# A fused attention and MLP kernel: setup, PSUM banks, planner's tables and last store changed

## The chip, the core and the metric

The kernel runs on one core of a Trainium2 chip. The metric is the device time of one launch in microseconds (us), the median of several runs; lower is better. Engines: PE (TensorE, matrix products into PSUM), DVE (VectorE), ACT (ScalarE), POOL (GpSimd) and SP, which here issues nearly all DMA transfers and, like every engine, takes its instructions strictly in order.

## The reference

Three blocks follow each other on a batch of 2, 768 positions, 8 heads of 64 (512 columns):

```python
scores = scale * q @ k^T - slope * dist        # keep: first n_global keys, or 0 <= i-j < n_local
a = softmax(where(keep, scores, -1e9)); x = a @ v
xn = (x - mean) / sqrt(var + 1e-6) * g_ln
x = x + relu(xn @ w_ch1) @ w_ch2               # 512 -> 2048 -> 512
h = relu(x^T @ w_tok1) @ w_tok2                # 768 -> 256 -> 768 over positions
u = x + h^T
out = u + relu(u @ w_ch1') @ w_ch2'            # 512 -> 1536 -> 512
```

`n_global` (8 here) and `n_local` (96 here) are inputs, so the kernel reads them at run time.

## The kernel before

The 1536 rows are 12 tiles `T` of 128 rows, six per batch row. `setup_consts` loads the two counts into one partition (`nwords`, one DMA on SP's queue, one on ACT's), spreads them to 128 partitions by a matmul with a row of ones (`nps`) and a copy (`both`), builds distances (`rel`, 512 columns, raised to a huge value where a key lies ahead of the query) and the first tile's masks, and computes a flag that says whether the fast path may run. In the meantime PE runs dummy matmuls (`keep_busy`). All engines then read the flag and branch. A second flag, read after the fast path, says whether a slow general path must run instead; a bounds check goes with each read.

In the fast path nothing is issued in the order of the code. Every operation is entered in a plan with engine, cost, priority, what it reads and writes and which buffers it takes; the planner (`Plan.order`) runs through the plan as a simulation and its order of starts is the order of instructions on each engine. Priorities come from tables of numbers (`SLOT`, `AHEAD`, `HEAD`, `DUE`, `LEAD` and others), and letters in other tables say which engine does a step (`EVX`, `PVE`, `LOA1`, `FE`, ...: A is ACT, V is DVE, G is GpSimd).

`window_tile` enters one tile of attention, four pairs `p` of heads. For a pair PE computes scores (`S`, L451), DVE adds the mask and takes the row's minimum (`low`, L468), ACT the exponential (`ex`, L473), PE turns the probabilities (`T`, L478), ACT or DVE copies them to SBUF (`pt`, L526 or L529), and PE multiplies by V (`PV`, L483), with a column of ones that gives the sum. For T below SPLIT, 6, the products are in fp32; two pairs share a PSUM bank of the pool `t`, and after each second pair DVE adds a small number to the sums, inverts them and scales 128x256 values into `x` (L537 to L539). For T from 6 the probabilities are split in two fp16 parts, and `PT` says pair by pair whether PE turns them (P) or a DMA transpose does (D).

Then a row tile is normalised (`xn`, `xh`), transposed by SP's DMA transpose into `xa` or `xb` (L591), and the MLPs run as three fp16 matmuls per product (L372 to L374). Weights come as raw words: `stg` is loaded (SP), ACT makes `fw` (L755), DVE `wf` (L761), and ACT with DVE or GpSimd the two fp16 parts `wa`/`wb` (L777, L780, L783); some are stored to DRAM (`scr_...`, L736) and reloaded later (L726). A guard checks value ranges; its tiles are cleared by GpSimd (L663).

PSUM has eight banks, two for each of the pools `m`, `s`, `t` and `k`; `BANKS` names the pool for each use. Results of tiles 0 to 9 are stored when they are done, tiles 10 and 11 (`BEHIND`) in a last block behind a prefetch hint for the second branch.

Of the kernel before, what the change touches and what calls it, by code (L numbers as in the profile page):

```python
# [22 lines left out]
P = 128  # L23
# [21 lines left out]
def setup_consts(o, tp):  # L45

    tc, nc, cp = o.tc, o.nc, o.cp
    w = tp.tile([1, 2, 2], I32, name="nwords")
    for i, n in enumerate((o.n_global, o.n_local)):
        (nc.sync, nc.scalar)[i].dma_start(w[:, i, :], n.bitcast(I32).rearrange("(o a) -> o a", o=1))  # L50
# [9 lines left out]
    ones = tp.tile([1, P], F32, name="ones")  # L60
    nc.vector.memset(ones[:], 1.0)
    idle = o.nps.tile([P, 256], F32, name="idle")
    keep_busy(o, idle, BUSY[0])
# [15 lines left out]
    neg = tp.tile([1, 2, 1], F32, name="neg")  # L79
    nc.vector.scalar_tensor_tensor(out=neg[:], in0=w[:, :, 0:1], scalar=0.0, in1=w[:, :, 1:2], op0=ALU.is_lt,  # L80
                                   op1=ALU.add)
    nval = tp.tile([1, 2, 1], F32, name="nval")
# [9 lines left out]
    ng, nl = nval[:, 0, :], nval[:, 1, :]  # L92
# [3 lines left out]
    both = cp.tile([P, 2], F32, name="both")  # L96
    nc.vector.tensor_copy(both[:], ps[:])
    o.ng, o.nl = both[:, 0:1], both[:, 1:2]
# [301 lines left out]
def window_tile(o, plan, prio, T, slot):  # L400
# [33 lines left out]
    if T >= SPLIT:  # L434

        ao = Buf("ao", lambda: o.sm.tile([P, H, 2, D + 1], F32, tag="ao", name="ao", bufs=2))
        sm = Buf("sum", lambda: o.sm.tile([P, H], F32, tag="sum", name="sum", bufs=3))
    mn = Buf("mn", lambda: o.sm.tile([P, H], F32, tag="mn", name="mn", bufs=3))
    x = o.x[T][:].rearrange("p (h d) -> p h d", h=H)
    for p in range(4):  # L440
        k = k0 + p
        if p % 2 == 0:
# [12 lines left out]
            if T < SPLIT:  # L455
                bv = psum_buf(o, "PV", [4, D + 1])
# [23 lines left out]
        def pv(p=p, pt=pt, bv=bv):  # L480
# [50 lines left out]
        if T < SPLIT:  # L531
            op("T", 2 * PVC * n, prio(k + slot["PV"]), pv, r=[(pt, 0), *vkeys], w=[(bv, p % 2)], get=[bv] if p % 2 == 0 else [])
        if T < SPLIT and p % 2 == 1:
            sm = Buf("sum", lambda: o.sm.tile([P, 4], F32, tag="sum", name="sum", bufs=3))

            def scale(p=p, bv=bv, sm=sm):
                nc.vector.tensor_scalar(out=sm.t[:], in0=bv.t[:, :, D], scalar1=1e-9, scalar2=None, op0=ALU.add)  # L537
# [4 lines left out]
            op("V", 0.7, prio(k + slot["inv"]), scale, r=[(bv, 0), (bv, 1)], w=[("x", T, p // 2)], get=[sm])  # L542
# [101 lines left out]
class Guard:  # L644
# [7 lines left out]
    def __init__(self, o, plan):  # L652
# [458 lines left out]
BANKS = {'L1': 'm', 'L2': 'm', 'L2S': 't', 'norm': 'k', 'chain': 'k', 'uT': 't', 'S': 's', 'T': 't', 'PV': 't', 'tok1': 's', 'tok2': 't'}  # L1111
# [5 lines left out]
def store(o, T):  # L1117
    b, t = divmod(T, NT)
    o.nc.sync.dma_start(o.out[b, t * P:(t + 1) * P, :], o.x[T][:])


def rest_pools(o, ctx):
# [15 lines left out]
    o.ps = {p: pool("ps" + p, o.sizes[p], space=PSUM) for p in PSUMS}  # L1138
# [3 lines left out]
def rest(o, ctx, attn, fast):  # L1142
# [136 lines left out]
LEADS, FLEAD = 25.19, 159.37  # L1279
F2LEAD = [-28.4, -27.06]  # L1280
FE, SE = 'VGVVVVGVVGVG', 'GVGGVVVV'
HEAD = 56.45
DUE = [32.72, 16.66, 78.81, 48.03]
EARLY = [42.85, -26.35, 1.23, -4.64]
LEAD = -178.69
EVAC = 20.66
TOK1 = 41.8
TOKW, TOK0 = 247.08, 102.37
# [5 lines left out]
class WindowAttention:  # L1294
# [8 lines left out]
    def ops(self, o, plan, prio):  # L1303
# [23 lines left out]
class GeneralAttention:  # L1327
# [7 lines left out]
    def attend(self, o, ctx):  # L1335
# [16 lines left out]
        for T in range(NTT):  # L1352
# [24 lines left out]
            for h in range(H):  # L1377
# [16 lines left out]
                acc = bank(o, "PV", 512)  # L1394
# [15 lines left out]
def mixer_kernel(ctx, tc, q, k, v, n_global, n_local, g_ln, w1, w2, wt1, wt2, w3, w4, out):  # L1410
# [20 lines left out]
    near = nc.values_load(flag[0:1, 0:1], min_val=0, max_val=1)  # L1431
# [5 lines left out]
    again = nc.values_load(o.again[0:1, 0:1], min_val=0, max_val=1)  # L1437
# [50 lines left out]
```

## Time and profile before

| | us |
|---|---|
| median of 3 runs | 547.12 (547.0 to 549.04) |
| profiled run, whole | 546.87 |
| profiled run, span of its instructions | 545.08 |
| PE busy | 532.0 |
| DVE, ACT, POOL busy | 408.6, 337.1, 163.2 |
| first weight matmul starts | 53.08 |
| last DVE operation starts | 538.77 |

The span runs from the first to the last instruction; 1.8 us lie outside it. Busy matmuls are pipelined, so a matmul's own duration (0.33 us for 384 columns) is longer than the distance to the next one (0.16). A wait is put down to the semaphore that came last.

### The profile page before, as it was taken

How to read it: one execution, taken by the hardware profiler on the slowest of the kernel's cores; microseconds unless marked ns; L12 is line 12 of the kernel's file. 1: busy time of each engine (PE TensorE's matmuls, PEld its weight loads, DVE VectorE, ACT ScalarE, POOL GpSimd, SP SyncE). 2: the span in 40 equal slices, each digit the busy share in tenths (PEclk: the TensorE clock that was granted, in tenths of full speed). 3: DMA queues.
4: the chain of work that ended last, by engine and by line, in shares of the span. 5: the costliest groups of instructions: out<-in, count | busy, mean ns of one | idle time of the engine just before them, and what ended most of it. 6: DMA issues, size and time to landing. Idle time of an engine off the chain costs nothing.

```text
span 545.1 us, 9103 instructions
## 1 busy us (share of the span) xinstructions
PE 532.0 (98%) x3132; PEld 299.7 (55%) x3132; DVE 408.6 (75%) x902; ACT 337.1 (62%) x760; POOL 163.2 (30%) x181
## 2 busy tenths in 40 slices
PE   7989999999999999999999999999999999999995
PEld 5866666666555555555555555455445545555542
DVE  6977998788699632788897898988987786655341
ACT  6988668786976433459948766576685545524210
POOL 2133221223132424253444245324343442220000
PEclk9998999999999999999999999999999999999999
DMA  8898977695998568277319793146745332302012
GB/s 242 267 232 238 294 209 182 202 259 164 208 234 237 207 174 231 97 240 244 97 39 192 186 267 110 40 136 210 268 121 158 92 133 68 113 1 78 2 40 82
DMA packets 99242, 89.81 MB, mean 165 GB/s; under 512 B 58484, under 2 KB 72820, under 8 KB 99188
## 3 DMA queue, kind: packets, MB, share of 16 engines
q1 hardware_dynamic: 99186, 89.15, 57.2%
q8 instruction: 26, 0.43, 0.3%
q14 instruction: 28, 0.23, 0.1%
q10 hardware_dynamic: 2, 0.00, 0.0%
HBM read 61.87 MB, written 17.83 MB: 146 GB/s over the span
## 4 chain that ended last, share of the span: by engine, by line
PE 84%; ACT 6%; DVE 4%; DMA 2%; SPq 1%; issue 1%; POOL 0%; ACTq 0%
PE L L372 11%; PE L L374 11%; PE L L373 11%; PE L2S L372 9%; PE L2S L374 9%; PE L2S L373 9%; PE chain L372 4%; PE chain L374 4%; PE chain L373 4%; PE S L451 3%; DMA stg<-in_moe_w_ch_dram 2%; PE tok L373 2%; PE tok L372 2%; PE tok L374 2%; ACT ex L473 2%; PE T L478 2%
## 5 line engine op out<-in xcount | busy, mean ns | idle before, releaser
L372 PE MATMUL L2S<-wb,h 128*128 128x512 f16 x228 | 86.4, 379 | 0.0
L373 PE MATMUL L2S<-wb,h 128*128 128x512 f16 x228 | 86.4, 379 | 0.0
L374 PE MATMUL L2S<-wb,h 128*128 128x512 f16 x228 | 86.4, 379 | 0.0
L900 DVE SCALAR_TENSOR_TENSOR x<-L2S,x 128x512 f32<-128x512 f32 x57 | 39.2, 688 | 43.0 <-PE L2S L374 42.9
L755 ACT ACTIVATE fw<-stg 128x512 f16<-128x512 bf16 x62 | 47.5, 777 | 20.1 <-DMA stg<-in_moe_w_ch_dram 16.2
L374 PEld LDWEIGHTS <-h 128*128 128x128 f16 x336 | 32.9, 98 | 39.6
L372 PEld LDWEIGHTS <-h 128*128 128x128 f16 x336 | 33.1, 98 | 35.7
L373 PEld LDWEIGHTS <-h 128*128 128x128 f16 x336 | 32.9, 98 | 35.8
L834 POOL TENSOR_TENSOR Q<-wa 128x512 f32<-128x512 f16 x18 | 25.6, 1422 | 74.8 <-DVE sz L834 55.2
L473 ACT ACTIVATE ex<-ex,mn 128x256 f32<-128x256 f32 (+1 forms) x96 | 41.3, 480 | 7.5 <-DVE mn L468 7.4
L761 DVE SCALAR_TENSOR_TENSOR wf<-stg,fw 128x512 uint32<-128x512 uint32 x62 | 45.0, 739 | 0.5 <-ACT fw L755 0.5
L834 POOL TENSOR_TENSOR Q<-Q 128x256 f32<-128x256 f32 x36 | 31.5, 874 | 32.6 <-DVE Q L834 31.2
L372 PE MATMUL L<-wb,h 128*128 128x512 f16 x108 | 40.9, 379 | 0.0
L373 PE MATMUL L<-wb,h 128*128 128x512 f16 x108 | 40.9, 379 | 0.0
L374 PE MATMUL L<-wb,h 128*128 128x512 f16 x108 | 40.9, 379 | 0.0
L372 PEld LDWEIGHTS <-wa 128*128 128x128 f16 x268 | 26.2, 98 | 20.4 <-issue 2.7
L374 PEld LDWEIGHTS <-wa 128*128 128x128 f16 x268 | 26.2, 98 | 17.3
L373 PEld LDWEIGHTS <-wa 128*128 128x128 f16 x268 | 26.2, 98 | 17.3
L364 DVE SCALAR_TENSOR_TENSOR h<-L,h 128x384 f16<-128x384 f32 x40 | 22.1, 553 | 17.4 <-ACT h L358 17.1
L372 PE MATMUL L<-xa,wa 128*128 128x384 f16 x104 | 34.0, 327 | 0.0
L373 PE MATMUL L<-xa,wa 128*128 128x384 f16 x104 | 33.9, 326 | 0.0
L374 PE MATMUL L<-xa,wa 128*128 128x384 f16 x104 | 33.9, 326 | 0.0
(235 smaller groups left out, 1341.2 us busy)
## 6 DMA issues: line engine op xcount, KB each, us to landing
stg<-in_moe_w_ch_dram SPq DMA_DIRECT2D x56, 512.0 KB, 5.5
wa<-scr_1a SPq DMA_DIRECT2D x24, 256.0 KB, 3.5
wb<-scr_1b SPq DMA_DIRECT2D x24, 256.0 KB, 3.6
scr_1a<-wa SPq DMA_DIRECT2D x16, 256.0 KB, 4.0
scr_1b<-wb SPq DMA_DIRECT2D x16, 256.0 KB, 3.8
K<-in_k_dram SPq DMA_DIRECT2D x12, 256.0 KB, 3.6
Q<-in_q_dram SPq DMA_DIRECT2D x12, 256.0 KB, 4.3
V<-in_v_dram SPq DMA_DIRECT2D x12, 256.0 KB, 4.3
```

Of the source, the lines that this page charges most:

```text
L364: nc.vector.scalar_tensor_tensor(out=lo(), in0=src(), scalar=0.0, in1=plain(hi()), op0=ALU.max, op1=ALU.subtract)
L372: nc.tensor.matmul(ps, ah, bh, start=first, stop=False, **k)
L373: nc.tensor.matmul(ps, ah, bl, start=False, stop=False, **k)
L374: nc.tensor.matmul(ps, al, bh, start=False, stop=last, **k)
L451: nc.tensor.matmul(bs[j].t[:, i, :w], o.Q[r, qs, p + i, :], o.K[r, slots, p + i, :], start=True, stop=True)
L473: nc.scalar.activation(out=ex.t[:, j, :w], in_=ex.t[:, j, :w], func=AF.Exp, bias=mn.t[:, h:h + 1], scale=-1.0)
L478: nc.tensor.transpose(bt.t[:, j, i, :], ex.t[:, j, i * P:(i + 1) * P], o.ident[:])
L755: op("A", 0.66, prio - 2, lambda: nc.scalar.activation(out=fw.t[:, :, 1], in_=stg.t[:, 4:2049:4].bitcast(BF16), func=AF.Copy, scale=2.0 if ...
L761: op("V", 0.6, prio - 1, lambda: nc.vector.scalar_tensor_tensor(out=raw().bitcast(U32), in0=stg.t.bitcast(U32)[:, 1:1024:2], scalar=13, in ...
L834: op(eng, {"G": 0.1 + n * 0.00227, "V": 0.07 + n * 0.00104}[eng], prio, lambda: e.tensor_tensor(out=out(), in0=a(), in1=b(), op=alu), lock ...
L900: n = op("V", 0.6, prio, lambda: nc.vector.scalar_tensor_tensor(out=x[:], in0=b.t[:], scalar=BACK if o.half else 1.0, in1=x[:], op0=ALU.mu ...
```

## The change

1. **Setup.** The counts go to all 128 partitions by DMA (`partition_broadcast`); `ones`, the `nps` matmul and the copy `both` are gone, and the 13 dummy matmuls run in one piece. `rel`'s maximum covers only the last 128 columns; the other 384 follow in a planned operation, `distant`, after tile 0's first scores. The temporary `mt` lies in an output tile.
2. **Banks.** The two banks of pool `k` become one tile `k2`. The fp32 PV of a whole tile fills both, taken at its first pair, and one scaling of 128x512 follows the last pair. The fp16 PV (`PV2`) stays in `t`.
3. **Clears.** The guard's and `vb`'s clears on GpSimd are ordered after tile 0's last pair has been masked.
4. **Tables.** Nearly all priorities and engine letters are new, among them `EVX` (tile 3's `pt` copies to DVE), `PVE` (all ACT), `PT`, `LOA1` to `LOT`.
5. **End.** Tile 10's store is issued at the head of the last block, tile 11's on ACT's queue. The flags are read without the bounds check.

```diff
@@ setup_consts
-    w = tp.tile([1, 2, 2], I32, name="nwords")
+    w = tp.tile([P, 2, 2], I32, name="nwords")
-        (nc.sync, nc.scalar)[i].dma_start(w[:, i, :], n.bitcast(I32).rearrange("(o a) -> o a", o=1))
+        (nc.sync, nc.scalar)[i].dma_start(w[:, i, :], n.bitcast(I32).rearrange("(o a) -> o a", o=1).partition_broadcast(P).rearrange("p o a -> p (o a)"))
-    keep_busy(o, idle, BUSY[0])
+    keep_busy(o, idle, BUSY)
-    ps = o.nps.tile([P, 2], F32, name="nps")
-    nc.tensor.matmul(ps[:], ones[:], nval[:, :, 0], start=True, stop=True)
-    keep_busy(o, idle, BUSY[1])
-    both = cp.tile([P, 2], F32, name="both")
-    nc.vector.tensor_copy(both[:], ps[:])
@@ distances
-    nc.vector.tensor_tensor(out=rel[:], in0=rel[:], in1=t[:], op=ALU.max)
+    nc.vector.tensor_tensor(out=rel[:, 3 * P:], in0=rel[:, 3 * P:], in1=t[:, 3 * P:], op=ALU.max)
@@ bank
-    t = o.ps[BANKS[use]].tile([P, 512], F32, tag=BANKS[use], name=use)
+    t = o.k2[:, next(o.kb)] if BANKS[use] == "k" else o.ps[BANKS[use]].tile([P, 512], F32, tag=BANKS[use], name=use)
@@ window_tile
+    bvs = [psum_buf(o, "PV", [4, D + 1]) for _ in range(2)] if T < SPLIT else None
...
-            op("T", 2 * PVC * n, prio(k + slot["PV"]), pv, r=[(pt, 0), *vkeys], w=[(bv, p % 2)], get=[bv] if p % 2 == 0 else [])
-        if T < SPLIT and p % 2 == 1:
+            op("T", 2 * PVC * n, prio(k + slot["PV"]), pv, r=[(pt, 0), *vkeys], w=[(bvs[p // 2], p % 2)], get=bvs if p == 0 else [])
+        if T < SPLIT and p == 3:
...
-                nc.vector.tensor_tensor(out=x[:, 2 * p - 2:2 * p + 2], in0=bv.t[:, :, :D], in1=sm.t[:].rearrange(
-                    "p (h o) -> p h o", o=1).to_broadcast([P, 4, D]), op=ALU.mult)
+                nc.vector.tensor_tensor(out=x.rearrange("p (b h) d -> p b h d", b=2), in0=v[:, :, :, :D], in1=sm.t[:].to_broadcast([P, 2, 4, D]),
+                                        op=ALU.mult)
@@ Guard
-                plan.op("G", 0.2, GUARD0, lambda i=i, a=a, b=b, y=y: nc.gpsimd.memset(c[:, i, a:b], y), w=[("lim", k, i)])
+                plan.op("G", 0.05, GUARD0, lambda i=i, a=a, b=b, y=y: nc.gpsimd.memset(c[:, i, a:b], y), r=[("first", 3, 1)], w=[("lim", k, i)])
@@ tables (two lines of some thirty)
-PT = 'PDPDPPPPDPDPPPPDDDDDDDDP'
+PT = 'PPDPPPPDDPDDDDPDDPPDDDDD'
-EVX = 'AAAAVVAAVAVA'
+EVX = 'AAAVVVAAAAAA'
@@ rest
+        store(o, BEHIND[0])
         for x in rest:
             x.fn()
-        for T in BEHIND:
-            store(o, T)
+        store(o, BEHIND[1], "scalar")
@@ mixer_kernel
-    near = nc.values_load(flag[0:1, 0:1], min_val=0, max_val=1)
+    near = nc.values_load(flag[0:1, 0:1], min_val=0, max_val=1, skip_runtime_bounds_check_because="a product of comparisons, 0 or 1")
```

The tables move instructions on every engine. Three places follow, each as it stood before and as it stands now.

PE, from the scores of the fifth tile (T = 4) to the first weight matmul. Before (`PV`, `T` and `S` as above, `wa` and `L` the first weight product):

```order
L483 MATMUL PV<-V,pt 128x65 x8
L478 MATMUL T<-ident,ex 128x128 x4
L451 MATMUL S<-K,Q 128x256 x4
L478 MATMUL T<-ident,ex 128x128 x4
L483 MATMUL PV<-V,pt 128x65 x8
L478 MATMUL T<-ident,ex 128x128 x4
L372 LDWEIGHTS wa
L372 MATMUL L_858<-xa,wa 128x384
```

After (`k_211` is a bank of the pair that PV now fills):

```order
L445 MATMUL S<-K,Q 128x256 x4
L470 MATMUL T<-ident,ex 128x128 x4
L475 MATMUL k_211<-V,pt 128x65 x8
L470 MATMUL T<-ident,ex 128x128 x8
L445 MATMUL S<-K,Q 128x256 x4
L475 MATMUL k_211<-V,pt 128x65 x8
L365 LDWEIGHTS wa
L365 MATMUL L_846<-xa,wa 128x384
```

The whole of the fifth tile's PV, its last transposes and the next tile's first scores now stand ahead of the first weight matmul.

ACT, the same stretch, from the copies of tile 3's probabilities to the exponentials of tile 4 (`pt`, `ex`, `xn`, `xh` and `fw` as above). Before:

```order
L777 ACTIVATE wb_758<-wf_745 128x512
L777 ACTIVATE wb_768<-wf_750 128x512
L526 ACTIVATE pt_753<-T_752 128x512
L473 ACTIVATE ex_765<-ex_765,mn_766 128x256 x2
L473 ACTIVATE ex_774<-ex_774,mn_766 128x256
L755 ACTIVATE fw2_204<-stg_61 128x512
L473 ACTIVATE ex_774<-ex_774,mn_766 128x256
L755 ACTIVATE fw0_62<-stg_61 128x512
L755 ACTIVATE fw1_63<-stg_61 128x512
L624 ACTIVATE xn_832<-x3_67,st_812 128x512
L473 ACTIVATE ex_822<-ex_822,mn_766 128x256 x2
L473 ACTIVATE ex_830<-ex_830,mn_766 128x256 x2
```

After:

```order
L465 ACTIVATE ex_715<-ex_715,mn_716 128x256 x2
L580 ACTIVATE xh_733<-xn_704 128x512
L465 ACTIVATE ex_726<-ex_726,mn_716 128x256 x2
L465 ACTIVATE ex_768<-ex_768,mn_716 128x256
L617 ACTIVATE xn_779<-x3_67,st_756 128x512
L465 ACTIVATE ex_768<-ex_768,mn_716 128x256
L465 ACTIVATE ex_783<-ex_783,mn_716 128x256 x2
L580 ACTIVATE xh_804<-xn_779 128x512
L751 ACTIVATE fw2_190<-stg_61 128x512
L773 ACTIVATE wb_822<-wf_802 128x512
```

Three `fw` conversions, two `wb` copies and the `pt` copy are no longer in this stretch; `fw` and `wb` begin again behind tile 4's last exponentials.

SP, the transfers between the second and the third transposed tile `xa`. Before:

```order
L546 DMA K<-in_k_dram 128x4x32
L160 DMA K<-in_k_dram 128x512
L158 DMA V<-in_v_dram 128x8x64
L160 DMA Q<-in_q_dram 128x512
L166 DMA stg<-in_moe_w_ch_dram 128x2048
L166 DMA stg<-in_moe_w_ch_dram 128x4x512 x2
L548 DMA V<-in_v_dram 32x8x64
L591 DMA_TRANSPOSE xa<-xh 128x8x128
```

After:

```order
L153 DMA Q<-in_q_dram 128x512
L151 DMA V<-in_v_dram 128x8x64
L732 DMA scr_1a_707<-wa 128x1024
L732 DMA scr_1a_722<-wa 128x1024
L732 DMA scr_1a_741<-wa 128x1024
L541 DMA V<-in_v_dram 32x8x64
L151 DMA V<-in_v_dram 128x8x64
L732 DMA scr_1a_766<-wa 128x1024
L539 DMA K<-in_k_dram 128x4x32
L153 DMA K<-in_k_dram 128x512
L584 DMA_TRANSPOSE xa<-xh 128x8x128
```

The three `stg` loads are gone from this stretch, and four stores of converted weights (`scr_1a<-wa`) now stand ahead of the third transpose.

## Rows read from the trace of the kernel before

**Rows 1.** The page, busy time: engine, us busy, share of the span, instructions

```profile
PE 532.0 (98%) x3132; PEld 299.7 (55%) x3132; DVE 408.6 (75%) x902; ACT 337.1 (62%) x760; POOL 163.2 (30%) x181
```

**Rows 2.** Windows: stretch, length, busy time (instructions) of each engine, TensorE clock, DMA, GB/s

```profile
20.00:40.00 20.00, 17.70 (x142) 14.45 (x141) 17.52 (x64) 18.42 (x39) 5.70 (x9) 1.00 0.91 239
40.00:60.00 20.00, 18.67 (x132) 14.49 (x131) 15.64 (x43) 15.06 (x31) 6.94 (x8) 0.91 0.93 249
100.00:120.00 20.00, 20.00 (x162) 13.12 (x161) 16.24 (x50) 16.87 (x41) 6.15 (x7) 1.00 0.67 196
```

**Rows 3.** PE's waits, 0 to 60 us: waiter, releaser, us in total, times, longest

```profile
PE PV L483 <- ACT pt L526: 3.2, 3, 1.6
```

**Rows 4.** The chain that ended last, 0 to 55 us: start, us, what

```profile
3.73 6.79 DMA stg<-in_moe_w_ch_dram
...
10.60 0.78 ACT fw L755
...
33.70 0.50 ACT pt L526
...
45.71 1.85 PE PV L483 x16
47.57 0.44 PE T L478 x4
48.01 1.06 PE S L451 x8
```

**Rows 5.** Timeline of PE: start, us, instruction and count, idle before and releaser

```profile
41.85 1.12 PE L478 MATMUL T<-ident,ex 128*128 128x128 f32 x4 [0.55 <-ACT ex L473]
...
52.41 0.84 PE L478 MATMUL T<-ident,ex 128*128 128x128 f32 x4 [0.48 <-ACT ex L473]
53.08 0.33 PE L372 MATMUL L<-xa,wa 128*128 128x384 f16 x1
```

**Rows 6.** Groups of instructions, 0 to 55 us: busy us, mean ns of one, idle before

```profile
L473 ACT ACTIVATE ex<-ex,mn 128x256 f32<-128x256 f32 x32 | 13.9, 497 | 0.0
L755 ACT ACTIVATE fw<-stg 128x512 f16<-128x512 bf16 x11 | 8.4, 774 | 3.3 <-DMA stg<-in_moe_w_ch_dram 3.3
L526 ACT ACTIVATE pt<-T 128x512 f32<-128x512 f32 x12 | 7.0, 581 | 0.7 <-PE T L478 0.6
L539 DVE TENSOR_TENSOR x<-PV,sum 128x256 f32<-128x256 f32 x9 | 3.8, 424 | 0.3
L777 ACT ACTIVATE wa<-wf 128x512 f16<-128x512 f32 x5 | 3.1, 622 | 0.0
L529 DVE COPY pt<-T 128x512 f32<-128x512 f32 x3 | 2.1, 688 | 0.5 <-PE T L478 0.5
```

**Rows 7.** SP's transpose of the third tile, and SP's longest waits

```profile
48.07 1.28 SPq L591 DMA_TRANSPOSE xa<-xh  x1
...
xa<-xh SPq DMA_TRANSPOSE x1, 3.3
...
SPq L166 <- DVE wf L761: 54.1, 21, 12.6
```

**Rows 8.** Timeline of the setup, DVE

```profile
2.69 0.69 DVE L125 TENSOR_TENSOR rel<-rel,mt 128x512 f32<-128x512 f32 x1
```

**Rows 9.** The end: timeline of DVE and SP; lines of the flag's branch; first store

```profile
538.77 0.69 DVE L900 SCALAR_TENSOR_TENSOR x<-L2S,x 128x512 f32<-128x512 f32 x1 [1.90 <-PE L2S L374]
...
539.49 0.33 SPq L1119 DMA_DIRECT2D out_dram<-x  x1
...
L1437 SPq TENSOR_LOAD <-flags x1: 441/441/441, 540.5 to 540.5; - x1
...
L1439 SPq EVENT_SEMAPHORE  x8: 17/17/17, 542.8 to 543.4; - x8
...
L1484 SPq EVENT_SEMAPHORE  x10: 17/28/28, 543.7 to 545.0; - x10
...
L50 ACTq DMA_DIRECT2D nwords<-in_n_local_dram x1: 507/507/507, 0.7 to 0.7; - x1
```

More of the change, by code (lines that the diff above doesn't have):

```diff
@@ L77, in setup_consts @@
         nc.scalar.memzero(fw[:])
-    neg = tp.tile([1, 2, 1], F32, name="neg")
+    neg = tp.tile([P, 2, 1], F32, name="neg")
     nc.vector.scalar_tensor_tensor(out=neg[:], in0=w[:, :, 0:1], scalar=0.0, in1=w[:, :, 1:2], op0=ALU.is_lt,
                                    op1=ALU.add)
-    nval = tp.tile([1, 2, 1], F32, name="nval")
+    nval = cp.tile([P, 2, 1], F32, name="nval")
     nc.vector.scalar_tensor_tensor(out=nval[:], in0=neg[:], scalar=2.0 ** 32, in1=w[:, :, 0:1], op0=ALU.mult,
@@ L116, in distances @@
     col = o.x[NTT - 2][:, :NGF].rearrange("p (o c) -> p o c", o=1)
-    t = tp.tile([P, 4 * P], F32, name="mt")
+    t = o.x[NTT - 4]
     nc.gpsimd.iota(ri[:, 3 * P:], pattern=[[-1, P]], base=0, channel_multiplier=1)
@@ L478, in probs, with pv @@
                     nc.tensor.transpose(bt.t[:, j, i, :], ex.t[:, j, i * P:(i + 1) * P], o.ident[:])
-        def pv(p=p, pt=pt, bv=bv):
+        def pv(p=p, pt=pt, bv=bvs and bvs[p // 2]):
             for j in range(2):
@@ L1114, with store @@
 SIZES = {**WIDE, 'hid': 12, 'wa': 8, 'wb': 8, 'wf': 4, 'fw': 3, 'stg': 4, 'xn': 2, 'ph': 3, 'pq': 2, 'xh': 2, 'uh': 2, 'xz': 3, 'sz': 4}
-def store(o, T):
+def store(o, T, queue="sync"):
     b, t = divmod(T, NT)
-    o.nc.sync.dma_start(o.out[b, t * P:(t + 1) * P, :], o.x[T][:])
+    getattr(o.nc, queue).dma_start(o.out[b, t * P:(t + 1) * P, :], o.x[T][:])
 def rest_pools(o, ctx):
@@ L1137, in rest_pools @@
     o.gp = pool("gp")
-    o.ps = {p: pool("ps" + p, o.sizes[p], space=PSUM) for p in PSUMS}
+    o.ps = {p: pool("ps" + p, 1 if p == "k" else o.sizes[p], space=PSUM) for p in PSUMS}
+    o.k2, o.kb = o.ps["k"].tile([P, 2, 512], F32, name="k2"), cycle((0, 1))
     o.kept = {}
@@ L1278 @@
 BLOCKS2 = [[(c, (0, 1)) for c in range(3)]] * 2
[L1279 to L1288, printed above, removed]
+LEADS, FLEAD = -147.14, 465.29
+F2LEAD = [-23.63, -18.43]
+FE, SE = 'VVGGVGGGVVVG', 'GVGVGVVV'
+HEAD = 61.61
+DUE = [45.35, 16.18, 74.67, 46.67]
+EARLY = [-52.76, -27.78, -0.42, -0.15]
+LEAD = -159.32
+EVAC = 16.72
+TOK1 = -2.58
+TOKW, TOK0 = 176.01, 198.45
 SLOW = dict(SLOT={'gk': -30.97, 'exp': 16.12, 'T': -15.37, 'PV': -13.48, 'inv': 9.01, 'st': 17.62, 'xn': 12.62, 'tr': 1.7}, HEAD=107.54, DUE=[32.9, 21.07, 45.09, 4.38], EARLY=[-15.89, -16.66, 3.92, -16.37], LEAD=21.63, EVAC=3.31,
@@ L1306, in ops, with distant @@
         window_tile(o, plan, lambda k: HEAD0 + k, 0, dict.fromkeys(SLOT, 0.0))
-        plan.op("G", 0.3, 20.0, lambda: nc.gpsimd.memset(o.vb[:, :, :, 0, D:], VSC), w=[("vb", z, 0) for z in range(3)])
-        plan.op("G", 0.5, 20.0, lambda: nc.gpsimd.memset(o.vb[:, :, :, 1, D:], 0.0), w=[("vb", z, 1) for z in range(3)])
-        plan.op("V", 1.25, HEAD0 + 8.0, lambda: may(o, o.bmt, o.col, o.x[NTT - 1][:, :3 * P], 0, 3, False), r=[("first", 1, 1)], w=[("rel",)], lock=True)
+        o.guard.begin()
+        plan.op("G", 0.1, 20.0, lambda: nc.gpsimd.memset(o.vb[:, :, :, 0, D:], VSC), r=[("first", 3, 1)], w=[("vb", z, 0) for z in range(3)])
+        plan.op("G", 0.1, 20.0, lambda: nc.gpsimd.memset(o.vb[:, :, :, 1, D:], 0.0), r=[("first", 3, 1)], w=[("vb", z, 1) for z in range(3)])
+        def distant():
+            sl = slice(0, 3 * P)
+            nc.vector.tensor_tensor(out=o.bmt[:, sl], in0=o.bmt[:, sl], in1=o.x[NTT - 4][:, sl], op=ALU.max)
+            may(o, o.bmt, o.col, o.x[NTT - 1][:, sl], 0, 3, False)
+        plan.op("V", 1.7, HEAD0 + 8.0, distant, r=[("first", 1, 1)], w=[("rel",)], lock=True)
         for (d, e, at), engs in zip(((0, 2, HEAD0 + 8.1), (2, 3, MASK2)), (MK1, MK2)):
@@ L1393, in attend @@
                     nc.scalar.activation(out=pT[:, c, :], in_=tp[:, 0, :], func=AF.Copy)
-                acc = bank(o, "PV", 512)
+                acc = bank(o, "PV2", 512)
                 for c in range(NT):
```

59 lines of the change are left out of this document (29 added, 30 removed).

## The prediction

> **What bounds the kernel now.** I read the page's busy times first, then the table of windows, then PE's waits, and last the chain that ended last. PE is busy 98% of the span [rows 1], so the time is PE's work plus what PE loses. The windows say where it loses: 17.70 of 20 us busy in 20 to 40, 18.67 in 40 to 60, and there the granted clock averages 0.91; in 100 to 120 it is 20.00 of 20 [rows 2], and PE's wait list has no entry after 60 us. Before the first weight matmul, which starts at 53.08 [rows 5], the work is attention, and PE runs it with gaps: its largest wait is for ACT's copies of the turned probabilities (3.2 us in three times) [rows 3]. The chain agrees: a weight load holds it from 3.73 to 10.52, and from 10.60 to 34.2 us it is ACT without a break, then a mixture of ACT and PE [rows 4]. The dip of the clock lies there too: behind waits for ACT four transposes at 41.85 take 1.12 [rows 5] where the chain has four in 0.44 at full speed [rows 4]; 2.4 GHz fell to 1.2.
>
> So the change can win in three places: by making ACT's stretch before 53 us shorter, by taking work from PE, and after DVE's last operation (538.77, 0.69 long), behind which 5.6 us of span remain [rows 9].
>
> **The setup.** It loses an `ones` clear, a matmul, a copy, and three quarters of `rel`'s maximum (0.69 on 512 columns [rows 8]; about 0.5 of it). That brings the branch and the first scores some 0.3 to 0.6 us forward. I cost it at nothing: ACT's 14th row is the `fw` at 10.60 in both orders, it waits for a load that landed at 10.52 [rows 4], and the loads ahead of it on SP stand in the same order. The cover is the load; were it gone, 0.3 to 0.6 us would be won. The two counts on 128 partitions are a few KB; they cost nothing that the rows can show. GpSimd's clears keep their place, right behind its branch, and nothing that PE needs waits for them.
>
> **ACT ahead of the first weight matmul.** I counted both orders from the `fw` at 10.60 to the exponential that the last transpose ahead of the weights needs. Copies `pt` of 128x512 go from 12 to 8 (tile 3's go to DVE): 4 x 0.581 = 2.3 less. `fw` conversions go from 11 to 8: 3 x 0.774 = 2.3 less. Weight copies `wa`/`wb` go from 8 to 5: 3 x 0.622 = 1.9 less. Two more exponentials, 2 x 0.497 = 1.0, and a mask of 0.1 come in [rows 6]. Together ACT has 5.4 us less ahead, so by ACT alone the last transpose, at 52.41 before [rows 5], could come at 47.0. The shed work is not gone: the conversions stand behind the first weight matmuls, where PE has work.
>
> On PE the order now has more ahead of the weights: eight further PV products (16 records, as each fp32 product is two: 1.85), four transposes (0.44) and four score products (1.06) [rows 4], 3.35 us that need not be done later. So the gain in front is 53.08 + 3.35 minus the new start of the first weight matmul. By ACT alone that start is 47.0 + 0.44 + 1.06 + 1.85 = 50.4: gain 6.0. At the other end it starts at 56.4 and nothing is won.
>
> DMA stands between. The first weight matmul needs the third tile's transposed row, a transpose on SP's queue issued at 48.07 and 3.3 us in flight [rows 7], so landed at 51.4. In SP's order, counted from the shapes, 12,160 KB stand up to and with it before, 12,481 after (four stores of `wa` come ahead, loads of `stg` go behind). The windows move 239 and 249 GB/s [rows 2], or 238 KB per us, so 321 KB put it 1.3 us later, at 52.7. I take 52.9, nearest to that row: **gain 3.5 us**, ends 0 and 6.0. The same pace gives the next narrow place. The first matmul of the second half's rows needs a reloaded `wa` at 20,225 KB, by 85.0 us; PE, with 67.7 us of work ahead of it at the spacings of the rows and 18 us lost till then (52.9 less 34.9 of work), comes at 85.7. It just holds, and a smaller loss in front than 17.3 would be given back here.
>
> **The pair of banks.** Twelve scalings of 128x256 (0.424 for the largest step) become six of 128x512, as long as a 128x512 copy, 0.688 [rows 6]: 12 x 0.424 = 5.1 against 6 x 0.688 = 4.1 on DVE, and the two small steps halve in number; DVE pays four more copies with it, 2.8. Off the path this is nothing. But the next tile's first PV now has to wait until the whole pair is scaled. In DVE's order the scaling stands ahead of the copy `pt` that this PV needs anyway, or beside ACT's, with transposes and scores (0.44 to 1.5 us) between two PV groups on PE; I cost it at 0, with 1.0 per tile over five tiles as the upper end. The Trainium skill (PSUM — Partial Sum Buffer, PSUM bank collisions raise a hardware error) has accesses guarded by bank, not address, so a PV into either bank may not run under the scaling; no row of before shows such a wait, and by it a late DVE would cost those 5 us in full.
>
> **Transposes.** `PT` moves PE transposes to the DMA: 132 become 122 on the fast path. At 0.44 for four [rows 4], 10 x 0.11 = **1.1 us** leave PE, in a stretch where PE never waits. Ends: 1.1, or 0 if the DMA transposes that replace them arrive late.
>
> **The end.** Before, SP issues the last store at 539.49, reads the flag at 540.5, and only from 542.8 goes through 8 and then 10 waits to 545.0 [rows 9]. After, the store is ACT's, so SP's flag, branch and waits run earlier; ACT does issue, flag and branch behind DVE instead, and its issue is longer (0.507 against 0.33 [rows 9]). ACT then has no list of waits: 543.7 minus 542.8 of the first list and the assertion go, 0.9, and part of the second, against 0.2 for the issue. I take **1.0 us**; ends 0 and 2.0. The Trainium skill (Trainium Kernel Development and Optimization, Key Constraints) says that queues of different engines share the same 16 DMA engines and that issuing from several saves only issue time; by that the store lands no earlier and only 0.3 us would be won, a total 0.7 higher. The rows speak against reading it so: SP's waits come a second and more after the issue and are not the transfer.
>
> **Sum.** 546.87 (profiled run, span 545.08) - 3.5 - 1.1 - 1.0 = 541.3; the median of the runs is 0.25 higher, so **541.5 us**. The unknown ends together give 541.5 - 2.5 - 1.0 = 538.0 to 541.5 + 3.5 + 1.1 + 1.0 = 547.1.
>
> **Rivals.** *The front wins nothing.* The 3.35 us more ahead of the weights just push their start to 56.4, because SP, which issues in order, now waits at the four stores for converted weights before it reaches the transpose. For it: SP has waited 54.1 us in 21 waits for DVE's `wf` [rows 7]. Against: those weights stand early in ACT's and DVE's orders. Time: 547.1 - 2.1 = 545.0.
>
> *ACT alone sets the front.* DMA closes its holes, PE runs at full clock to the weights: gain 6.0, 2.5 more than forecast: 539.0. Against it is the pace, even in both windows.
>
> *PE waits at the pair of banks.* Up to 5 x 1.0 given back: 541.5 + 5.0 = 546.5. For it: DVE is busy 17.52 of 20 us in 20 to 40 [rows 2]; against: the place in DVE's order.
>
> *Slower: the reloads come late.* Three `fw` and three weight copies were moved behind the first weights; `stg` is freed by them, SP waits for it in order, and the reloaded `wa` at 20,225 KB stands behind. If it lands 8.4 us later, at 94.1, PE stops there and the time is 549.9; that takes a pace of 215 KB per us, 220 GB/s, over the first 94 us. Windows have 239 and 249, but 100 to 120 only 196 [rows 2], so it is near enough. With a half-clock stretch behind the stop, about 551.
>
> *The change doesn't do what it says at the start:* the setup's gain is hidden by the load at 10.52. That is in the forecast already.
>
> **How the numbers follow.** Forecast 0.53 (its own range 539.5 to 544), ACT alone 0.10, front wins nothing 0.20, banks 0.06, late reloads 0.11. What a measurement can tell is about 0.5%, 2.7 us: faster is below 544.4, slower above 549.9. Forecast and ACT alone give faster, 0.63; the front that wins nothing and the banks give same, 0.26; late reloads slower, 0.11. The range reaches from ACT alone to the banks, 538.5 to 546.8, and leaves out the slow case and some of the edges.
>
> **What would show it.** The first weight matmul near 52.9 with these three groups of attention ahead of it, no window below 1.00 of the clock, ACT's `fw` still at 10.6, SP's waits at the end over before ACT's. Wrong would be a weight matmul after 55 us, PE waiting for DVE's `sum` at a PV, PE waiting for `wa` between 80 and 95 us, or an end still 5.6 us behind DVE's last operation.

## The result, and the profile after

The changed kernel takes **552.53 us** (median of 20 runs, 550.57 to 559.77). The kernel before took 547.83 beside it (20 runs, 544.82 to 551.82). The ratio is 1.0089, 95% interval 1.007 to 1.0107: **slower by about 0.9%**, 3.8 to 5.9 us. The forecast was 541.5, range 538.5 to 546.8.

The profiled run took 554.85 us, 2.3 above the median, with a span of 553.0. The page and the windows, in the columns of [rows 1] and [rows 2]:

```profile
PE 535.7 (97%) x3118; PEld 302.2 (55%) x3118; DVE 417.0 (75%) x874; ACT 339.5 (61%) x764; POOL 172.4 (31%) x188
```

```profile
0.00:20.00 20.00, 14.35 (x98) 11.01 (x99) 11.65 (x57) 12.38 (x36) 2.80 (x30) 1.00 0.85 244
20.00:40.00 20.00, 18.70 (x149) 15.43 (x149) 15.62 (x56) 19.13 (x41) 7.46 (x10) 1.00 0.76 236
40.00:60.00 20.00, 17.23 (x102) 14.60 (x102) 14.30 (x45) 10.55 (x21) 6.32 (x9) 0.76 0.81 192
100.00:120.00 20.00, 20.00 (x148) 12.27 (x147) 13.99 (x36) 16.34 (x42) 3.96 (x4) 1.00 0.81 219
```

ACT did become idle in 40 to 60 (10.55 us busy, 15.06 before), yet PE did less there (17.23 against 18.67) and the granted clock fell further (0.76 against 0.91). PE's largest waits over the whole span (waiter, releaser, us in total, times, longest) are three that the forecast did not have:

```profile
PE S L445 <- DVE x L142: 4.6, 1, 4.6
PE k L365 <- DVE h L357: 1.7, 3, 0.6
PE k L475 <- DMA V<-in_v_dram: 1.7, 1, 1.7
```

**The first of them is the setup.** The transfers of 0 to 12 us (operation, count, KB each, median us from issue to landing), then DVE's and PE's timelines, as [rows 5]:

```profile
nwords<-in_n_local_dram ACTq DMA_DIRECT2D x1, 1.0 KB, 5.2
nwords<-in_n_global_dram SPq DMA_DIRECT2D x1, 1.0 KB, 6.0
```

```profile
6.82 0.16 DVE L78 SCALAR_TENSOR_TENSOR neg<-nwords 128x2 f32<-128x2 int32 x1 [3.83 <-DMA nwords<-in_n_global_dram]
```

```profile
8.60 1.22 PE L445 MATMUL S<-K,Q 64*128 64x128 f32 x8 [4.59 <-DVE x L142]
```

The counts are on their way for 5.2 and 6.0 us, DVE stands 3.83 us for them, and the first scores start at 8.60, where they started at 5.05. ACT's first `fw`, at 10.60 before, comes behind a copy that waits for PE's late transposes, and does not wait for its load:

```profile
12.32 0.38 ACT L518 ACTIVATE pt<-T 128x256 f32<-128x256 f32 x1 [0.89 <-PE T L470]
12.60 0.78 ACT L751 ACTIVATE fw<-stg 128x512 f16<-128x512 bf16 x1
```

The chain that ended last (start, us, what), led in [rows 4] by a weight load and then by ACT, begins with this load. In the stretch ahead of the weights it ends in PE's own work:

```profile
0.74 5.97 DMA nwords<-in_n_global_dram
...
38.48 4.35 DMA V<-in_v_dram
...
54.00 3.31 PE k L475 x16
57.30 1.71 PE T L470 x8
59.01 1.92 PE S L445 x8
60.93 1.93 PE k L475 x16
62.86 0.16 PE L L365
```

PE's timeline has the first weight matmul at 62.70:

```profile
62.70 0.33 PE L365 MATMUL L<-xa,wa 128*128 128x384 f16 x1
```

Before, it was at 53.08 [rows 5], and the order puts 3.35 us more ahead of it, so 6.3 us are lost there. Sixteen PV records take 3.31 where the same take 1.93 seven us later: at 54 the granted clock is 1.2 GHz instead of 2.4. PE had waited 1.69 us for V at 42.87 and 1.08 us for DVE at 52.28; the clock was low for 3.4 us from 43.6 and for 6.8 us from 53.9. Before, it was low once, 3.4 us from 41.8.

**The second lies 300 us later.** PE's timeline near 363 us, then DVE's:

```profile
362.50 0.33 PE L367 MATMUL L<-u,wa 128*128 128x384 f16 x1
363.40 0.32 PE L365 MATMUL k<-fx,sz 128*128 128x384 f16 x1 [0.58 <-DVE h L357]
```

```profile
362.79 0.56 DVE L357 SCALAR_TENSOR_TENSOR h<-k,h 128x384 f16<-128x384 f32 x1 [0.80 <-ACT V L952]
```

The step from 362.50 to 363.40 is 0.90 us where two such products are 0.16 apart: 0.74 lost, and the same again at 465.0 and 504.5. DVE's `h` reads one bank of the pair `k2`, PE's next product goes into the other. Since both are one tile, the reader counts as a reader of both; `e3` below tests this.

One number for each kernel helps below: PE's lost time, the time at which some amount of its work is done less that work at full-clock spacings, added up from PE's rows of the trace. Dummy matmuls don't count as work. The number is from one execution of each kernel and holds what low clock that one met; those of `e1` and `e3` took 4.3 and 1.9 us longer than their medians. After 5, 34.8 (nearly all attention that the changed kernel has ahead of the weights), 100 and 513 us of work:

| kernel | 5 | 34.8 | 100 | 513 |
|---|---|---|---|---|
| before | 10.5 | 21.4 | 22.4 | 23.7 |
| after | 13.3 | 27.9 | 28.9 | 34.0 |
| counts as before (`e1`) | 11.9 | 25.6 | 26.5 | 31.6 |
| banks apart (`e3`) | 13.3 | 27.3 | 28.6 | 30.4 |
| both (`e4`) | 9.9 | 21.7 | 23.1 | 24.9 |

**The end** did what was forecast: DVE's last operation starts at 547.77 and ends 0.69 later, and 4.5 us of span remain, 5.6 before [rows 9].

### The profile page after: what moved, and what is told of

It is laid out like the page before. It is cut to its first block, busy times and chain, and to the rows that moved or that the text cites. A ratio compares the mean times of both kernels' runs of the same rounds, so it can differ in the third digit from the quotient of the medians.

```text
span 553.0 us, 9011 instructions
## 1 busy us (share of the span) xinstructions
PE 535.7 (97%) x3118; PEld 302.2 (55%) x3118; DVE 417.0 (75%) x874; ACT 339.5 (61%) x764; POOL 172.4 (31%) x188
## 4 chain that ended last, share of the span: by engine, by line
PE 88%; DVE 5%; DMA 3%; ACT 2%; issue 1%; POOL 0%; DVEq 0%; POOLq 0%
PE L L365 12%; PE L L367 12%; PE L L366 12%; PE L2S L366 9%; PE L2S L367 9%; PE L2S L365 9%; PE k L365 4%; PE S L445 4%; PE k L367 4%; PE k L366 4%; PE k L475 4%; PE T L470 2%; PE tok L365 1%; PE tok L367 1%; PE tok L366 1%
## 5 line engine op out<-in xcount | busy, mean ns | idle before, releaser
L830 POOL TENSOR_TENSOR Q<-Q 128x256 f32<-128x256 f32 x36 | 32.9, 915 | 54.8 <-DVE Q L830 54.0
L465 ACT ACTIVATE ex<-ex,mn 128x256 f32<-128x256 f32 (+1 forms) x96 | 41.7, 479 | 12.3 <-DVE mn L460 12.2
L830 POOL TENSOR_TENSOR Q<-wa 128x512 f32<-128x512 f16 x18 | 26.3, 1459 | 60.9 <-DVE sz L830 56.4
L357 DVE SCALAR_TENSOR_TENSOR h<-L,h 128x384 f16<-128x384 f32 x40 | 22.2, 556 | 20.0 <-ACT h L351 19.6
L445 PE MATMUL S<-K,Q 64*128 64x256 f32 (+1 forms) x192 | 28.5, 406 | 6.3 <-DVE x L142 4.6
L460 DVE CUSTOM_DVE_ANT_0 ex<-bmh,S 128x256 f32<-128x256 bf16 x80 | 29.9, 413 | 6.2 <-PE S L445 4.7
L365 PE MATMUL L<-xa,wa 128*128 128x384 f16 x104 | 34.0, 327 | 0.0
```

Of the source, the lines that this page charges most:

```text
L357: nc.vector.scalar_tensor_tensor(out=lo(), in0=src(), scalar=0.0, in1=plain(hi()), op0=ALU.max, op1=ALU.subtract)
L365: nc.tensor.matmul(ps, ah, bh, start=first, stop=False, **k)
L445: nc.tensor.matmul(bs[j].t[:, i, :w], o.Q[r, qs, p + i, :], o.K[r, slots, p + i, :], start=True, stop=True)
L460: nc.vector.tensor_tensor_reduce(out=ex.t[:, j, :w], in0=o.bm0[:, h] if n == 1 else o.bmh[:, h, ms, :], in1=bs[j].t[:, p % 2, :w], scale=- ...
L465: nc.scalar.activation(out=ex.t[:, j, :w], in_=ex.t[:, j, :w], func=AF.Exp, bias=mn.t[:, h:h + 1], scale=-1.0)
L830: op(eng, {"G": 0.1 + n * 0.00227, "V": 0.07 + n * 0.00104}[eng], prio, lambda: e.tensor_tensor(out=out(), in0=a(), in1=b(), op=alu), lock ...
```

## The experiments

The theory after this reading: the broadcast counts and the one-tile pair of banks together are the loss. Its rivals: the tables moved the front wrongly (the load of V, or DVE in ACT's place). The last column is the ratio less one, times 548 us, with its interval; kernels are compared in it with runs of the kernel before on the same chip. `e1` to `e4` ran on one chip, the later ones on others, so across the two groups this column counts, not the medians. "Counts" is the part of the diff under `setup_consts`, "banks" the one under `bank` and `scale`.

| run | from | median | against before, us |
|---|---|---|---|
| after | | 552.53 | +4.9 (3.8 to 5.9) |
| `e1_old_counts` | after | 548.03 | -0.2 (-1.7 to 1.3) |
| `e2_new_counts_in_old` | before | 549.83 | +1.9 (0.2 to 3.6) |
| `e3_banks_apart` | after | 549.45 | +1.2 (-0.4 to 2.7) |
| `e4_both` | after | 545.10 | -3.8 (-5.3 to -2.4) |
| `e5_end_only` | before | 547.00 | -1.0 (-2.3 to 0.3) |
| `e6_old_tables` | `e4` | 547.09 | -0.4 (-1.5 to 0.7) |
| `e7_counts_to_32` | before | 549.75, one run | |
| `e8_no_global_v` | `e4` | 544.29 | -3.7 (-5.2 to -2.4) |
| `e9_low_parts_off_dve` | `e4` | 555.48 | +6.8 (4.2 to 9.4) |
| `e10_copies_in_old` | before | 547.80 | +0.5 (-1.2 to 2.3) |
| `e11_copies_back` | `e4` | 550.29 | +2.9 (1.2 to 4.7) |
| `e12_short_low_parts` | `e4` | 544.52 | -4.4 (-5.9 to -3.0) |

**The counts.** `e1` is the changed kernel with the counts loaded to one partition and spread by the matmul again, `e2` the old kernel with the new load:

```diff
-    w = tp.tile([P, 2, 2], I32, name="nwords")
+    w = tp.tile([1, 2, 2], I32, name="nwords")
+    nc.tensor.matmul(ps[:], ones[:], nval[:, :, 0], start=True, stop=True)
```

> The changed kernel with the counts loaded as before: into one partition, spread by the matmul and the copy; all else as changed. Theory S (the load of the counts to 128 partitions, which landed 5.97 us after its issue, holds up the branch and the loads behind it, and the later half-clock stretches are its consequence): the first scores come at about 5 us instead of 8.6, the first weight matmul moves from 62.9 to about 56, the time falls by about 6 us, to 546.5. Rival T (the new order of tables and the pair of banks lose the time in front by themselves): the first scores come at 5 us, but half-clock stretches between 40 and 61 us stay, and the time falls by 2.8 to 3.5 us at most, to 549.

> The kernel before with the counts loaded to 128 partitions (no ones, no matmul, no copy), nothing else changed. Theory S: the load lands some 5 us later than before, first scores near 8.5 instead of 5.05, ACT's first fw some 2 to 3 us later than 10.60, and the time rises by 3 us or more, to 551. Rival (the setup is hidden behind the first weight load, as the prediction had it): ACT's first fw stays at 10.6 and the time is the same within 0.5 us.

`e1` gains 4.5 us on the changed kernel, between theory S (6) and rival T (2.8 to 3.5); its first scores start at 4.65. Its first weight matmul, which S put at 56, comes at 60.47 in the profiled run, which has 10.2 us of low clock as the changed kernel's has, 3.4 from 11.2 and 6.8 from 41.9. So this trace doesn't bear out the second part of S, that the load brings the half-clock stretches. `e2` costs 1.9 us, where S had 3 or more, and shows the same wait:

```profile
PE S L444 <- DVE x L142: 4.6, 1, 4.6
```

So the load is the cause of the late start in both, at a different price. The scores start 3.6 to 4.1 us later in either; after 5 us of work the old kernel has lost 2.1 us by it (12.6 against 10.5), the new one 1.4 (changed kernel against `e1`) or 3.4 (`e3` against `e4`), and 2.3 or 5.6 by the first weights. In the first of these pairs both runs have 10.2 us of low clock, in the second it is 10.2 against 3.4, which at half clock is 3.4 us of the 5.6. So the wait itself costs some 2.2 us by the first weights, an estimate from these four runs. The median granted clock over all runs tells the rest: 0.994 in the changed kernel and 0.997 in `e1`, 0.992 in `e3` and 0.996 in `e4`, but 0.993 in the kernel before and 0.9925 in `e2`. With the new tables the load goes with a lower clock, with the old ones it doesn't. In the kernel before, 0.016 of clock goes with some 6 us (last section), so 0.003 to 0.004 would be 1.1 to 1.5 us, again an estimate. The old kernel had a wait there already, for ACT behind the weight load of [rows 4].

`e7` loads to 32 partitions, with only the first one used:

```diff
-    w = tp.tile([1, 2, 2], I32, name="nwords")
+    w = tp.tile([32, 2, 2], I32, name="nwords")
```

> The kernel before with the counts loaded to 32 partitions instead of one; the rest of the setup uses one of them as before, so 31 rows do nothing. Theory N (the packets are made one after the other, some 0.03 us each, and the loads behind wait for them): 64 packets instead of 256, the count's load lands some 1.2 us later than with one partition, at 2.4 to 3.3 us, and the first scores come at 5.05 to 5.5. Rival (a load that repeats its source costs a fixed time): it lands at 6 to 7 us, first scores near 8.

Its transfers (as above) land in 2 us, and the first scores start at 5.05 as before:

```profile
nwords<-in_n_local_dram ACTq DMA_DIRECT2D x1, 0.2 KB, 2.0
nwords<-in_n_global_dram SPq DMA_DIRECT2D x1, 0.2 KB, 1.9
```

A load that repeats its source is therefore not slow by itself; the landing time grows with the number of partitions. The bytes grow with them, 8 to each, but a first load of K of 256 KB lands 2.7 us after its issue in the kernel before, so they are not the reason. The time of that one run, 549.75, holds 13.7 us of low clock from 40.1 on and decides nothing.

**The banks.** `e3` is the changed kernel with two tiles of one bank, and the scaling in two pieces:

```diff
-    o.k2, o.kb = o.ps["k"].tile([P, 2, 512], F32, name="k2"), cycle((0, 1))
+    o.k2, o.kb = [o.ps["k"].tile([P, 512], F32, name=f"k{i}", tag=f"k{i}") for i in range(2)], cycle((0, 1))
```

> The changed kernel with the pool k as two tiles of one bank each instead of one tile of two; the scaling of a tile stays at the same place in DVE's order, as one inversion and two steps of 128x256. Theory F (three waits of PE for DVE's h in the stages from 360 us on, 0.74 us lost at each, come of the two banks being one tile, so that a matmul into one waits for a reader of the other): these three waits vanish, the time falls by 2.2 us, to 550.3. Rival: they are waits on the same bank; they stay and the time is the same or, with two more DVE steps a tile, up to 1 us longer.

> Both: the changed kernel with the counts loaded as before and the two banks as two tiles. If S and F hold and add up: 552.5 - 6 - 2.2, about 544.3, 3 us below the kernel before. If T holds for the front: 547. If neither holds: 549 to 552.

`e3` gains 3.1 us; PE has no wait left after 300 us, and from 100 to 513 us of work it loses 1.8 us instead of 5.1. `e1`, with one tile, still has the three waits:

```profile
PE k L372 <- DVE h L364: 1.7, 3, 0.6
```

`e4`, with both undone, takes **545.10 us and beats both kernels**: 7.4 us under the changed one, ratio to the old one 0.9931 (0.9904 to 0.9957). The two parts add up: 4.5 and 3.1 singly, 4.35 and 2.9 each beside the other.

**The end alone** (`store(o, BEHIND[1], "scalar")` and the unchecked flags put into the old kernel):

> The kernel before with the change of the end alone: tile 10's store ahead of the last DVE operation, tile 11's on ACT's queue, flags read without the bounds check. Theory E (SP's flag, branch and waits were the end): from DVE's last operation to the end of the span 4.2 to 4.5 us instead of 5.6, the time 1.1 to 1.4 us shorter, 546.7. Rival (queues of two engines share the transfer engines and only the issue is saved): 0.3 us. A second rival: ACT's longer issue and its own flag and branch take SP's place, 0.

DVE ends 4.9 us ahead of the span's end, 5.6 before; the time, 1.0 lower, isn't clear of zero.

**The tables.** `e6` is `e4` with all tables of the kernel before.

> The changed kernel with counts as before and banks apart, and with all priorities and engine letters of the kernel before (30 tables), so that setup split, pair of banks for PV and end are the change that is left. Theory P (the new tables bring ten PE transposes less, 1.1 us, and nothing in front): 1 us above the same kernel with the new tables, 546.2. Rival Q (the tables were made for the pair of banks, and the old ones make PE wait for the scaling at each tile): 548 or more, with waits of PV for DVE's sum. Rival R (the new tables cost time in front): 544 or less.

They are worth 3.4 us by the last column (2.0 by the medians), and little ahead of the weights: PE's lost time after 34.8 us of work is 21.6, in `e4` 21.7, of which 1.7 is low clock that `e6`'s run did not have. Ten transposes fewer are 1.1 of it by the forecast's price. Behind the first weights, at 88.29, PE waits once for DVE in `e6`, for which `e4` waits 0.2 us in all:

```profile
PE L L372 <- DVE h L364: 1.6, 1, 1.6
```

The kernel before, with the old tables too, has no such wait, so it belongs to the old tables with the new banks. Together that is 2.5; the rest stays unassigned.

**Why the front gains nothing.** In `e4` the first weight matmul starts at 56.58, that is 53.08 + 3.5: the forecast's rival "the front wins nothing", which gave 56.4. `e8` takes out the small loads of V's first rows, for which PE waits 1.3 us in `e4`:

> The changed kernel with counts as before and banks apart, and without the small load of the first rows of V (32 rows, 64 KB) into each tile's V for tiles below 6; the products with those global keys are therefore not the reference's. Theory V (in front PE now waits for these loads, which SP issues late because they wait for PE's previous PV, and which stand behind three weight loads on the queue: 4.41 us in flight, PE idle 1.3 us, then a half-clock stretch): the wait and the half clock at 41 us vanish, the first weight matmul comes at about 53.5 instead of 56.6, the time falls by 3 us to 542. Rival W (DVE's and ACT's chain through mask, exponential and copy is right behind): the first weight matmul comes at 56 and the time falls by under 1 us.

Rival W holds: -0.8 us by the medians, 0.1 longer by the last column. The first weight matmul starts at 55.68, 0.9 earlier, and a low-clock stretch of 3.4 us stays, from 36.2: the hole is worth itself at most. `e10` makes one part of the tables alone, tile 3's copies on DVE; `e11` takes it back in `e4`:

```diff
-EVX = 'AAAAVVAAVAVA'
+EVX = 'AAAVVVAAVAVA'
```

> The kernel before with one letter changed, the four pt copies of tile 3 on DVE instead of ACT. If ACT's sum of work set the front, as the prediction had it: 2.3 us less on ACT, the first weight matmul up to 2.3 us earlier, time 545.5. Theory D: DVE gets 2.8 us more and takes the place of ACT, the time is the same within 1 us or longer.

> The changed kernel with counts as before and banks apart, and the four pt copies of tile 3 back on ACT. If ACT's sum set the front: 2.3 us longer, 547.4. Theory D: DVE's 2.8 us leave and ACT waits less, the time is the same within 1 us or shorter, 544 to 545.

`e10` relieves ACT by the copies: its first weight matmul starts at 49.02, with sixteen PV records and four transposes (2.3 us by the forecast's prices) moved behind it, and PE has lost 19.6 us after 34.8 us of work, 1.8 less than before. After 100 us of work it is 22.8 against 22.4: the gain is given back at once behind the front. `e11` loses 6.7 us against `e4` by the last column (5.2 by the medians), most of it between 100 and 200 us of work and so not in the front: one letter moves the planner's whole order, and this run does not price the copies. In both kernels with the copies on DVE, ACT waits for DVE instead; its longest wait ahead of 58 us, of `e10` and then of `e4`:

```profile
ACT ex L473 <- DVE mn L468: 3.2, 3, 2.0
```

```profile
ACT ex L472 <- DVE mn L467: 5.8, 3, 2.5
```

The kernel before has no such wait of ACT. From that of `e4` I formed theory D: DVE has taken ACT's place as the bound. `e9` moved five of DVE's weight steps to GpSimd:

```diff
+        moved = o.w64 and o.half and src[:2] == (1, "a") and src[2] < 5
+        if moved:
+            lo_eng = "G"
```

> The changed kernel with counts as before and banks apart, and with the low parts of the first five wa tiles made on GpSimd (a subtraction without the scale, so these weights are not the reference's) instead of DVE: five times 0.69 us leave DVE, in the stretch before and around the first weight matmul. Theory D (what ACT was relieved of, DVE took over: ACT now waits 5.8 us for DVE's masked scores between 38 and 58 us): PE's loss up to the first weight matmul falls by 1.5 us or more, the time by as much, to 543.5. Rival L (it is the round trip PE, DVE, ACT, PE, no engine's load): the time stays within 0.7 us of 545.1.

It tells nothing on D: the planner made another order, and 9 us went between 100 and 200 us of work. `e12` repeats the test without moving any instruction:

```diff
+            short = o.w64 and o.half and src[:2] == (1, "a") and src[2] < 10
-            op("V", 0.6, prio, lambda: nc.vector.scalar_tensor_tensor(
+            op("V", 0.6, prio, (lambda: nc.vector.tensor_scalar(
+                out=dst()[1], in0=dst()[0], scalar1=0.0, scalar2=None, op0=ALU.mult)) if short else lambda: nc.vector.scalar_tensor_tensor(
```

> The kernel with counts as before and banks apart, in which VectorE's low parts of the first ten first-layer weights (0.68 us each, about nine of them ahead of the first weight matmul) are replaced by a product of the fp16 high part with zero, so that only the fp16 part of these weights counts; the order of instructions is the same on every engine. Theory D (VectorE has taken ACT's place as the bound of the front): the operations shrink by some 0.3 to 0.5 us each, about 3 to 4 us in all, ACT's waits for mn (5.8 us) fall to under 4, the first weight matmul starts 2 to 3.5 us before 56.6, and the time falls from 545.1 to 542 to 543.5. Rival (the front is held by the weights' own arrival and by the chain through all engines): the first weight matmul moves by under 1 us and the time by under 0.8. If the replacement is not shorter than 0.6 us, the run tells nothing.

Five of the ten low parts lie ahead of the first weights. Their group on DVE ahead of 57 us (operation, shape, groups | busy us, mean ns | idle before), of `e4` and of `e12`:

```profile
L787 DVE SCALAR_TENSOR_TENSOR wa<-wf,wa 128x512 f16<-128x512 f32 x5 | 4.7, 943 | 0.5 <-ACT wa L781 0.5
```

```profile
L788 DVE TENSOR_SCALAR wa<-wa 128x512 f16<-128x512 f16 x5 | 2.1, 417 | 0.9 <-ACT wa L781 0.9
```

DVE has 2.6 us less to do, and the first weight matmul starts at 56.77 instead of 56.58; ACT's wait for `mn` is 6.2 instead of 5.8; the time, 544.52, is 0.6 lower, inside the rival's bound. **Theory D falls too.** The chain of `e4` in front of the weights:

```profile
34.69 4.41 DMA V<-in_v_dram
39.09 0.04 issue
39.14 1.78 PE k L482 x14
40.92 1.48 PE T L477 x8
42.40 2.01 PE S L452 x8
44.41 1.98 PE k L482 x16
...
48.59 1.13 PE S L452 x6
49.72 0.59 PE T L477 x4
50.31 1.94 PE k L482 x16
```

PV, scores and transposes are 35.5, 16.9 and 16.4% of this chain from 17 to 56 us; the rest is loads, waits and steps of other engines. The windows of the same stretch, of the kernel before and then of `e4` (columns as in [rows 2]), and PE's waits in it, before and then in `e4`, show what became of the relief:

```profile
17.00:56.00 39.00, 35.38 (x267) 28.26 (x265) 32.57 (x115) 34.37 (x71) 12.75 (x19) 0.96 0.88 237
17.00:56.00 39.00, 35.19 (x259) 28.14 (x258) 31.72 (x107) 29.68 (x60) 13.75 (x19) 0.96 0.82 224
```

```profile
PE PV L483 <- ACT pt L526: 1.6, 2, 1.2
PE T L478 <- ACT ex L473: 1.0, 2, 0.6
PE PV L483 <- DMA V<-in_v_dram: 0.7, 2, 0.5
PE PV L483 <- DVE st L610: 0.3, 1, 0.3
```

```profile
PE k L482 <- DMA V<-in_v_dram: 1.3, 1, 1.3
PE S L452 <- DVE mn L467: 1.1, 1, 1.1
PE k L482 <- ACT pt L525: 0.8, 2, 0.6
PE T L477 <- ACT ex L472: 0.5, 1, 0.5
```

ACT has 4.7 us less to do, nearly the 5.4 of the forecast, and PE is busy as long as before at the same granted clock. Its waits changed hands: 2.6 us for ACT became 1.3, and V and DVE took over the rest. `e8` and `e12` take from V and from DVE alone, and the first weight matmul moves by 0.9 us at most. What would have to go together to shorten the front stays open. PE's busy time also hides some loss: `e4` runs 46 dummy matmuls behind 5 us, the last at 26.4, some 0.11 us each, about 5 us.

## Why the prediction was wrong

**"The two counts on 128 partitions are a few KB; they cost nothing that the rows can show."** This step failed most: 4.5 us of the 11 between forecast and result. It was costed by bytes. I named the cover, the `fw` at 10.60 which waits for a load landed at 10.52 [rows 4], but did not ask whether the cover moves: the first weight load stands behind the counts on the same queue and landed at 12.2. Nor is it the load that holds the `fw` now; at 12.60 it stands behind PE's late transposes. That DVE's first setup operation waits for the counts stood in the code; between 0 and some microseconds for a load no row had, the upper end was never set. The setup's own gain of 0.3 to 0.6 was right in size: `e4`, with the shorter `rel` and the old counts, starts its scores at 4.67, 0.4 earlier.

**"I cost it at 0" (the pair of banks).** I looked for the wait where the pair is filled, at the PV of tiles 0 to 5. None stands there: PE's list has no wait for the scaling. But the pool `k` also serves the token MLP's chain products 300 us later, and there the one tile made false waits: 3.1 us, of which the three waits are 2.2. The step that failed is the question "who else uses this buffer"; the upper end of 5.0 held by luck, for another mechanism. The rule of the Trainium skill (PSUM — Partial Sum Buffer, PSUM bank collisions raise a hardware error) that the prediction drew on is about two accesses to one bank. Here they are in two banks, and the wait goes away when only the tile is split (`e3`).

**"Gain 3.5 us" in front.** The counts were right: in `e4`, without the two causes above, ACT loses 4.7 us from 17 to 56 us. The inference wasn't: there the first weight matmul starts at 56.58, a gain of -0.15. The step that failed lets ACT's 5.4 us pass into PE's start until the third transpose, at 52.7, stops it. PE's idle time stayed at 3.6 to 3.8 us of 39, ended by V and DVE in ACT's place. Nor was the transpose the stop: it landed at 54.5 in `e4`, 2 us ahead of the first weight matmul, and PE has no wait for it. A sign stood in [rows 2]: PE was busy 17.70 and 18.67 of 20, so 3.6 us of idle and some 1.7 of clock could be given back besides dummy matmuls, and that idle was ended by ACT, DVE and loads in turns. The rival with 0.20 had the front's number, 56.4, but its reason, SP waiting at the four stores for converted weights, is 0.6 us of waits for `wa` ahead of 62 us in `e4`.

**Transposes, 1.1 us:** 132 became 122 without a new wait above 0.4 us; nothing contradicts it, and `e6` against `e4` has room for it. **The end, 1.0 us:** behind DVE's last operation the span is shorter by 1.1 in the changed kernel, 1.4 in `e4` and 0.7 in `e5`, each from one execution; in the time of `e5` it isn't clear of zero. The Trainium skill (Trainium Kernel Development and Optimization, Key Constraints) has issuing from several engines save only issue time. The 0.3 us by that reading is too small in all three. (SP's waits that the prediction puts "a second and more" behind the issue are a microsecond and more behind it.)

**The slower rival** (reloads late between 80 and 95 us) did not happen: PE has no wait for `wa` there. The time came out slower by two causes of which I had priced neither as a loss, so the 0.11 for slower rested on the wrong mechanism.

**The sum in hindsight:** against the kernel before, tables -2.0 and end -1.0 or so; counts +4.5, banks +3.1. That is +4.6; the medians differ by 4.7. Each term has an interval of 1 to 2 us either way, so that they meet this closely is luck. Nor are the old tables alone 2.0 us slower, as `e6` pairs them with the new banks. Of the counts' 4.5 us, by the estimates above, some 2.2 are the wait and 1.1 to 1.5 low clock; the rest is within the interval. Why the load goes with a lower clock under the new tables only stays open.

## What to carry to other kernels

Cost a load by its packets and by who waits for the first word, not by its bytes; then ask whether what hides it is queued behind it. When buffers become one tile, list every user of that pool in the whole program, not only the one that the change is for. Relief of a busy engine is worth no more than what the engine that sets the end loses in that stretch, and next to nothing if several engines end its idle time in turns: here 4.7 us less on ACT left PE's idle time as it was.

## What the runs showed of the hardware

- **Tiny packets.** A load of 8 bytes to each partition landed in 1.2 to 1.3 us for one partition, 1.9 and 2.0 for 32, and 5.2 to 6.0 for 128. Single packets took 7 to 9 ns, but those of one load to 128 partitions started over 3.8 us; why they are so far apart isn't shown. The Trainium skill (DMA: Bandwidth & Descriptors, Specifications) gives 512 bytes as the smallest transfer at line rate. The trace agrees in direction: 1 KB took longer than 256 KB of K. It also shows that the first loads behind on the queue come later: the first K, issued at 1.2 in both, took 6.2 us instead of 2.7, and the first weight load landed at 12.2 instead of 10.5.
- **The clock.** The granted clock fell to 1.2 GHz shortly after PE had waited in front, in stretches of 3.4 to 13.7 us; in the changed kernel at 43.6, after a wait that ended at 42.87, and at 53.9, after one that ended at 52.28. It need not: `e6`'s profiled run waits 1.17 us in front and stays at 2.4 GHz. One kernel's runs follow it: runs of the kernel before at a mean granted clock of 0.997 take about 545 us, at 0.981 about 551. A microsecond of waiting in that place can so cost more than itself, and differences under 2 us there need many runs.
